# Attention and GEGLU block on one core: batch 1's queries and keys in token rows, weights in thirds, a new order in batch 0

## The chip, the cores and the metric

The kernel runs on one core of one Trainium2 chip. The metric is the device time of one execution in microseconds (us): 375.97 as the median of six runs (374.69 to 376.41). Engines are named as in the profile: PE is TensorE (PEld its weight loads), DVE is VectorE, ACT is ScalarE, POOL is GpSimd, SP is SyncE. Differences under about 0.3% are taken as no change.

## The reference

Eight batches of eight heads, 576 tokens, head size 64; each batch has 16 "beacon" keys and values that every token may see, ahead of 576 causal ones. The attention's output, put together as 4608 tokens by 512, goes through a gated block with three weight matrices.

```python
k_all = np.concatenate([beacon_k, k], axis=2)
v_all = np.concatenate([beacon_v, v], axis=2)
scores = scale * np.matmul(q, k_all.transpose(0, 1, 3, 2))
scores = np.where(causal, -1000000000.0, scores)
a = np.exp(scores - scores.max(-1, keepdims=True))
a /= a.sum(-1, keepdims=True) + 1e-09
x = np.matmul(a, v_all)                 # then transposed to (4608, 512)
g, val = x @ w_gate, x @ w_val          # (4608, 1536) each
out = (gelu(g) * val) @ w_out           # (4608, 512), float32
```

## The kernel before

All matrices are brought to bf16 by the loads themselves. GpSimd issues every load (`dma`, line 115, and the weights, lines 170 and 173), in program order, in the same queue in which it also runs its masks; SyncE issues the stores, the DMA turns of queries and keys (`transpose_dma`, line 232) and of attention output (`turn_dma`, line 365). The order of the instructions on every engine is the program's own: `keep` holds them in the order in which they are written.

**Attention of a batch.** Heads are taken in four pairs m = 0 to 3, the two heads of a pair in the two halves of the partitions. `qkT` holds turned queries and keys (head size down the partitions). For a pair, `scores` computes four chunks (0 to 3, widths 512, 480, 464, 208 a head) of keys by queries into one of two buffers of `psum_s`, and ScalarE writes their exponentials to `exp_ring`. Causal masks are added by small matmuls in batch 0 (`score_mms`, the `eye`/`neg` pairs) and made by GpSimd on the exponentials from batch 1 on (`masks`, line 292, at the end of `scores`): chunk 0 has key tile t = 0, chunk 1 tiles 2 and 4, chunk 2 tile 1, chunk 3 tile 3. `attend` (30 matmuls against values with a column of ones, x_ps) and `normalize` (DVE) follow; both together are `av`. `turn` turns the result y on TensorE and `put` copies it to `xT_sb`; pairs 0 and 1 of batches 1 to 7 are turned by DMA instead.

**The gated block.** Tokens go in nine chunks of 512. `gate_val` is one block of 128 of the 1536 columns: four matmuls for the gate and four for the value (gv_ps, 8 x 512 columns), gelu on ScalarE, product on DVE into `hT_sb`. `out_mms` accumulates the output of 128 tokens over twelve of these. Chunk b's gate/value blocks follow attention b; the output matmuls of chunk b - 1 are spread between the pieces of attention b (`o(n)` is n of them). In the last gate/value block of a chunk ("tx") the gate half is in `psum_t`, the value half in `psum_x`. The PSUM banks are `psum_s` (two buffers of two banks), `psum_x` (two banks), `psum_t` and `psum_o` (one each).

**Queries and keys.** They reach the kernel in rows of 64 elements a head and token. Batches 2 to 7 are loaded in that form (`qk_loads`, 11 loads a batch), 128 tokens to the partitions, into two rings by b % 2, and turned by DMA. Batches 0 and 1 (`NPERM` = 2) are loaded six tokens to a partition (`load_qk6`: runs of 384 elements, 96 partitions, into a buffer shared with `hT_sb`) and turned by TensorE: a half turn (`transpose_half`, w = 1 for keys, 0 for queries) is 12 turns of 96 x 64, for keys one more for the beacons, and one or two copies by DVE (by ScalarE for the first queries). Batch 1's half turns of pairs 0 to 2 stand between the gate/value blocks 5 to 10 of batch 0, that of pair 3 (`transpose_pe`) behind the first two score chunks of batch 1.

**The order around the change.** Loads: queries and keys of batch 0 by pairs; values of batch 0; gate and value weights in column blocks 0-2, 2-4, 4-8, 8-12, with the first half of batch 1's queries and keys ahead of the last of these; the second half; out weights in one load; values of batch 1. In batch 1, batch 2's 11 loads are put out in part by `ahead(2)` at two places between score chunks, the other seven behind the attention. In batch 0's attention, both half turns of a pair stand together, chunks go in twos (`c(m, *AB)` is chunks 0 and 2, `*CD` 1 and 3), two filler matmuls (`warm(2, ...)`, line 522) stand before pair 2's last two chunks, and `av` of pairs 0 to 2 stands between the chunks of pair 3.

Of the kernel before, what the change touches and what calls it, by code (L numbers as in the profile page):

```python
# [7 lines left out]
P = 128  # L8
B, H, S, NB, D = 8, 8, 576, 16, 64
SK = S + NB  # L10
# [5 lines left out]
CH = 512  # L16
N_CHUNKS = N_TOK // CH
NPAIR = H // 2
NPERM = 2
MASKED = -1e6  # L20


# [16 lines left out]
AB, CD = (0, 2), (1, 3)  # L39
# [14 lines left out]
def kernel(  # L54
# [14 lines left out]

    const = ctx.enter_context(tc.tile_pool(name="const", bufs=1))  # L70
    ring = ctx.enter_context(tc.tile_pool(name="ring", bufs=1))
    npool = ctx.enter_context(tc.tile_pool(name="npool", bufs=2))
    fpool = ctx.enter_context(tc.tile_pool(name="fpool", bufs=3))
    hpool = ctx.enter_context(tc.tile_pool(name="hpool", bufs=2))
    opool = ctx.enter_context(tc.tile_pool(name="opool", bufs=2))
# [38 lines left out]
    def dma(out_ap, in_ap):  # L114
        keep(nc.gpsimd.dma_start(out=out_ap, in_=in_ap))  # L115

    qk6 = {}

    def qk6_of(b):
        if b not in qk6:  # L120
            qk6[b] = (
                hpool.tile([P, 2, H, 6 * D], BF16, name="qk6", tag="hT_sb"),
                npool.tile([NB, H, D], BF16, name="kb", tag="kb"),
            )
        return qk6[b]

    def load_qk6(b, h0, h1, ws=(1, 0)):
        for w in ws:
            src = (q, k)[w]
            dma(  # L130
                qk6_of(b)[0][0:96, w, h0:h1, :],
                src[b, h0:h1, :, :].rearrange("h (p r) d -> p h (r d)", r=6),
            )

    def load_kb(b):
        dma(qk6_of(b)[1], beacon_k[b].rearrange("h t d -> t h d"))

    def key_loads(src, beacon, dst, b):
        parts = [
            (dst[0:NB, 0, :, :], beacon[b].rearrange("h t d -> t h d")),  # L140
            (dst[NB:P, 0, :, :], src[b, :, 0:112, :].rearrange("h p d -> p h d")),
        ]
# [4 lines left out]
        return [lambda o=o, i=i: dma(o, i) for o, i in parts]  # L147

    def qk_loads(b):
        q_sb, k_sb = q_ring[b % NRING], k_ring[b % NRING]  # L150
# [8 lines left out]
    def load_qk(b):  # L159
        for load in qk_loads(b):  # L160
            load()

    def load_v(b):
        for load in key_loads(v, beacon_v, v_ring[b % NRING][:, :, :, 0:D], b):
            load()

    def load_gate_val(f0, f1):
# [4 lines left out]
    def load_out_w():  # L172
        keep(nc.gpsimd.dma_start(out=wo_sb, in_=moe_w_out.rearrange("(ii p) m -> p ii m", p=P)))

    def mm(out_ap, lhsT, rhs, start, stop, **kw):
        keep(nc.tensor.matmul(out_ap, lhsT, rhs, start=start, stop=stop, **kw))  # L176
# [5 lines left out]
    def tr(out_ap, in_ap):  # L182
        n = in_ap.shape[0]
        keep(nc.tensor.transpose(out_ap, in_ap, ident[0:n, 0:n]))  # L184

    def tr_part(b, m, w, dst):
        qk, kb = qk6[b]
        for r in range(6):
            for hi in range(2):
                tr(  # L190
                    dst[64 * hi : 64 * hi + 64, r * 96 : (r + 1) * 96],
                    qk[0:96, w, 2 * m + hi, r * D : (r + 1) * D],
                )
        if w:
            tr(dst[:, S:SK], kb[:, 2 * m : 2 * m + 2, :])

    def transpose_pe(b, m):
        t_ps = psum_x.tile([P, 2, 1024], BF16, name="t_ps", tag="x")
        for w in range(2):
            tr_part(b, m, w, t_ps[:, w, :])  # L200
        keep(
            nc.vector.tensor_copy(
                qkT[:, m, :, NB:SK].rearrange("p w (t r) -> p w t r", r=6),
                t_ps[:, 0:2, 0:S].rearrange("p w (r t) -> p w t r", r=6),
            )
        )
        keep(nc.vector.tensor_copy(qkT[:, m, 1, 0:NB], t_ps[:, 1, S:SK]))

    def transpose_half(b, m, w, by_act=False):
        pool, tag = ((psum_o, "o"), (psum_t, "t"))[w]  # L210
        t_ps = pool.tile([P, 1024], BF16, name="t_ps", tag=tag)
        tr_part(b, m, w, t_ps)
        out_ap = qkT[:, m, w, NB:SK].rearrange("p (t r) -> p t r", r=6)
        in_ap = t_ps[:, 0:S].rearrange("p (r t) -> p t r", r=6)
        if by_act:
            act(out_ap, in_ap, ACT.Copy)
        else:
            keep(nc.vector.tensor_copy(out_ap, in_ap))  # L218
        if w:
            keep(nc.vector.tensor_copy(qkT[:, m, 1, 0:NB], t_ps[:, S:SK]))  # L220

    def warm(n, pool, tag):
        w_ps = pool.tile([P, D_MODEL], FP32, name="w_ps", tag=tag)
        for j in range(n):
            mm(w_ps, idle[:, 128 * (j % 4) : 128 * (j % 4) + 128], idle, True, True)
# [228 lines left out]
            if fi == F_TILES - 1:  # L454
                out_store(ci, ti, o_of[ci][1])

    kb_sb = opool.tile([NB, H, D], FP32, name="kb_sb", tag="o_sb")
    keep(nc.sync.dma_start(out=kb_sb, in_=beacon_k[0].rearrange("h t d -> t h d")))
    load_qk6(0, 0, 2)
    load_qk6(0, 2, 4, (1,))  # L460
    keep(
        nc.gpsimd.affine_select(
            out=eye,
# [5 lines left out]
            channel_multiplier=-1,  # L469
        )  # L470
    )
    load_qk6(0, 2, 4, (0,))
    keep(
        nc.gpsimd.affine_select(
            out=neg,
# [17 lines left out]
    load_qk6(1, 4, H)  # L493
    load_out_w()
    load_v(1)

    def av(b, m, where="x"):
# [9 lines left out]
    keep(nc.vector.tensor_copy(qk6[0][1], kb_sb))  # L507
    transpose_half(0, 0, 1)
    transpose_half(0, 0, 0, by_act=True)
# [24 lines left out]
    av(0, 3, "s")  # L534
    turn(0, 2)
    put(0, 2, by_act=True)
    keep(nc.scalar.preload_act_table_set(SET_GELU))
    gv_mms(0, 0, 0, 1)
    turn(0, 3, psum_o, "o")
    put(0, 3)  # L540
    gv_mms(0, 1, 0, 1, where="x")
    for kk in (2, 3):
        for fi in (0, 1):
            gv_mms(0, fi, kk, last=kk == 3)
    for b in range(B):
        u = [0]

        def o(n):
            out_mms(b - 1, u[0], u[0] + n)
            u[0] += n  # L550

        def ahead(n):
            for _ in range(n):
                if loads:
                    loads.pop(0)()

        loads = qk_loads(b + 1) if b == 1 else []
        if b:
            keep(nc.scalar.preload_act_table_set(SET_EXP))
            o(4)  # L560
            scores(b, (0, 0))
            scores(b, (0, 2))
            if b == 1:
                transpose_pe(1, 3)
            o(7)
            scores(b, (0, 1))
            scores(b, (0, 3), (1, 3))
            ahead(2)
            o(7)
# [24 lines left out]
            av(b, 3)  # L594
            keep(nc.scalar.preload_act_table_set(SET_GELU))
            gv_mms(b, 0, 0, 1, 2)
            gv_mms(b, 1, 0)
            turn(b, 3)
            put(b, 3)
            gv_mms(b, 1, 1, 2)  # L600
            gv_mms(b, 0, 3, last=True)
            gv_mms(b, 1, 3, last=True)
        for fi in range(F_TILES):
            if fi >= 2:
                gate_val(b, fi, "x" if b and fi == 2 else "tx" if fi == F_TILES - 1 and b < B - 1 else "s")
            if b == 0 and 5 <= fi < 11:
                transpose_half(1, (fi - 5) // 2, (fi - 4) % 2)
            if fi == 0:
                ahead(len(loads))
                if b and b + 1 < B:  # L610
                    load_v(b + 1)
                if b and b + 2 < B:
                    load_qk(b + 2)
                if NPERM <= b + 1 < B:
                    transpose_dma(b + 1)
    for fi in range(F_TILES):
        gate_val(N_CHUNKS - 1, fi)
# [37 lines left out]
```

## Time and profile before

| | |
|---|---|
| median of 6 runs | 375.97 us |
| the profiled execution | 374.69 us, span 373.0 us, granted TensorE clock 1.00 |
| TensorE busy | 364.1 us, 98% |
| GpSimd / ScalarE / VectorE busy | 158.9 / 187.8 / 152.0 us |
| DMA moved by GpSimd's queue | 19.13 MB (bf16 bytes) |
| third gate/value block of batch 0 starts | 27.06 us |
| output matmuls of chunk 0, 1, 2 start | 47.55, 87.88, 129.49 us |
| out weights: issued, landed after | 28.28 us, 17.8 us |

The span runs from the first to the last instruction. A line of the timeline gives the start, the duration, the engine, the line of the code, the operation, what it writes and reads, and in brackets the idle time before it with what ended that. Matmuls are pipelined, so a group's duration reaches some 0.17 us beyond the start of what follows; lengths of stages are better taken from start to start. From batch 3 on, one batch takes 39.72 us (129.49 to 169.21 and so on).

### The profile page before, as it was taken

The page shows a single profiled execution, that of the slowest core. Times are in us where ns is not written, and L with a number is a line of the kernel's source. Part 1 is how long each engine was busy: PE and PEld are TensorE (multiplying, and loading weights), DVE is VectorE, ACT ScalarE, POOL GpSimd, SP SyncE. Part 2 cuts the span into 40 slices and gives each one's busy share as a digit, 9 for nine tenths or more (in the row PEclk, how much of TensorE's full clock was granted, in tenths as well). Part 3 has the DMA queues.
Part 4 walks back from the last instruction along what each step waited for, and adds up shares of the span by engine and source line. Part 5 has one row for each costly group of instructions (what it writes and reads, how often), then busy time and mean ns, then how long its engine had stood idle before and what let it go on. Part 6 is the DMA issues. An engine that isn't in the chain of part 4 may idle for free.

```text
span 373.0 us, 7487 instructions
## 1 busy us (share of the span) xinstructions
PE 364.1 (98%) x3032; PEld 180.9 (49%) x3032; DVE 152.0 (41%) x257; ACT 187.8 (50%) x241; POOL 158.9 (43%) x282
## 2 busy tenths in 40 slices
PE   7899999998999999999999999999999999999996
PEld 3664445543454446444554455445544464444443
DVE  3454644442344425433444335333444244424332
ACT  4963277335753487338733774358534873332210
POOL 8935046974467245843495148614600330000000
PEclk9999999999999999999999999999999999999999
DMA  8999959999569923999299929991591030000102
GB/s 104 169 204 204 194 58 117 151 130 150 69 122 144 151 41 91 159 136 85 60 148 154 80 77 127 138 128 47 120 157 20 33 87 30 0 0 30 56 34 109
DMA packets 149826, 38.33 MB, mean 103 GB/s; under 512 B 136352, under 2 KB 145312, under 8 KB 149792
## 3 DMA queue, kind: packets, MB, share of 16 engines
q0 software_dynamic: 104960, 19.13, 68.9%
q1 hardware_dynamic: 44832, 18.73, 26.6%
q8 instruction: 24, 0.39, 0.5%
q14 instruction: 10, 0.08, 0.1%
HBM read 38.27 MB, written 9.44 MB: 128 GB/s over the span
## 4 chain that ended last, share of the span: by engine, by line
PE 89%; DMA 4%; ACT 2%; SPq 2%; POOL 1%; issue 1%; DVE 0%
PE gv_ps L176 42%; PE o_ps L176 25%; PE s_ps L176 8%; PE x_ps L176 8%; DMA qkT<-q_sb 2%; SPq L232 2%; ACT expT L179 2%; PE t_ps L184 1%; PE g_ps L176 1%; PE v_ps L176 1%; DMA k_sb<-in_k_dram 1%; PE y_ps L184 1%; PE w_ps L176 1%; POOL k_sb L115 1%; DVE y_sb L344 0%
## 5 line engine op out<-in xcount | busy, mean ns | idle before, releaser
L179 ACT ACTIVATE ge_sb<-gv_ps 128x512 bf16<-128x512 f32 x101 | 59.4, 597 | 134.2 <-PE gv_ps L176 134.2
L179 ACT ACTIVATE expT<-s_ps 128x960 bf16<-128x960 f32 (+2 forms) x114 | 101.8, 947 | 28.1 <-PE s_ps L176 24.6
L419 DVE TENSOR_TENSOR hT_sb<-gv_ps,ge_sb 128x512 bf16<-128x512 f32 x101 | 69.1, 690 | 106.2 <-ACT ge_sb L179 106.2
L176 PE MATMUL gv_ps<-xT_sb,wg_sb 128*128 128x512 bf16 x404 | 107.8, 379 | 0.0
L176 PE MATMUL gv_ps<-xT_sb,wv_sb 128*128 128x512 bf16 x404 | 107.7, 379 | 0.0
L176 PE MATMUL o_ps<-wo_sb,hT_sb 128*128 128x512 bf16 (+2 forms) x444 | 105.9, 374 | 0.0
L292 POOL TENSOR_SCALAR_AFFINE_SELECT expT<-expT 128x256 bf16<-128x256 bf16 (+2 forms) x140 | 51.7, 385 | 114.4 <-ACT expT L179 107.0
L176 PEld LDWEIGHTS <-wv_sb 128*128 128x128 bf16 x432 | 42.2, 98 | 51.0
L176 PEld LDWEIGHTS <-wg_sb 128*128 128x128 bf16 x432 | 40.8, 98 | 46.1
L176 PEld LDWEIGHTS <-hT_sb 128*128 128x128 bf16 x444 | 38.8, 98 | 46.3 <-issue 8.8
L438 DVE COPY o_sb<-o_ps 128x512 f32<-128x512 f32 (+2 forms) x37 | 25.0, 676 | 45.9 <-PE o_ps L176 45.8
L176 PE MATMUL s_ps<-qkT 64*128 64x336 bf16 (+5 forms) x384 | 35.0, 282 | 3.6 <-DMA qkT<-q_sb 1.8
L176 PEld LDWEIGHTS <-expT 128*128 128x128 bf16 (+1 forms) x960 | 32.2, 97 | 7.8 <-issue 2.3
L115 POOL DMA_DIRECT2D v_sb<-in_v_dram x40 | 33.7, 868 | 4.0 <-DMA wg_sb<-in_moe_w_gate_dram 1.6
L176 PE MATMUL x_ps<-v_sb,expT 128*128 128x65 bf16 x930 | 33.8, 193 | 0.5 <-issue 0.5
L115 POOL DMA_DIRECT2D k_sb<-in_k_dram x30 | 25.2, 846 | 20.1 <-DMA q_sb<-in_q_dram 10.8
L176 PEld LDWEIGHTS <-qkT 64*128 64x128 bf16 x384 | 14.3, 94 | 24.5 <-issue 20.8
L344 DVE TENSOR_TENSOR y_sb<-x_ps,r_sb 128x640 bf16<-128x640 f32 x31 | 25.5, 824 | 1.4 <-PE y_ps L184 0.4
L115 POOL DMA_DIRECT2D q_sb<-in_q_dram x30 | 25.4, 895 | 0.0
L342 DVE RECIPROCAL r_sb<-x_ps 128x10 f32<-128x10 f32 x31 | 6.8, 221 | 40.4 <-PE x_ps L176 40.4
L218 DVE COPY qkT<-t_ps 128x576 bf16<-128x576 bf16 x13 | 9.7, 751 | 5.9 <-PE t_ps L184 5.9
L377 DVE COPY xT_sb<-y_ps 128x576 bf16<-128x576 bf16 x16 | 7.3, 457 | 11.5 <-PE y_ps L184 11.5
(50 smaller groups left out, 120.9 us busy)
## 6 DMA issues: line engine op xcount, KB each, us to landing
out_dram<-o_sb SPq DMA_DIRECT2D x35, 256.0 KB, 2.2
v_sb<-in_v_dram POOLq DMA_DIRECT2D x24, 128.0 KB, 6.5
q_sb<-in_q_dram POOLq DMA_DIRECT2D x24, 128.0 KB, 9.3
k_sb<-in_k_dram POOLq DMA_DIRECT2D x18, 128.0 KB, 9.4
wo_sb<-in_moe_w_out_dram POOLq DMA_DIRECT2D x1, 1536.0 KB, 17.8
wg_sb<-in_moe_w_gate_dram POOLq DMA_DIRECT2D x2, 512.0 KB, 11.8
wv_sb<-in_moe_w_val_dram POOLq DMA_DIRECT2D x2, 512.0 KB, 13.8
v_sb<-in_v_dram POOLq DMA_DIRECT2D x8, 112.0 KB, 4.3
```

Source lines behind the costliest of these rows:

```text
L115: keep(nc.gpsimd.dma_start(out=out_ap, in_=in_ap))
L176: keep(nc.tensor.matmul(out_ap, lhsT, rhs, start=start, stop=stop, **kw))
L179: keep(nc.scalar.activation(out_ap, in_ap, func, **kw))
L184: keep(nc.tensor.transpose(out_ap, in_ap, ident[0:n, 0:n]))
L218: keep(nc.vector.tensor_copy(out_ap, in_ap))
L232: nc.sync.dma_start_transpose(out=qkT[:, :, w, c + j * P : c + j * P + n], in_=src[0:n, j, :, :].rearrange("p h d -> p (h d)"),)
L292: nc.gpsimd.affine_select(out=d, in_=d, pattern=[[0, 2], [1, n]], compare_op=ALU.is_ge, fill=0.0, base=NB if t == 0 else 0, channel_multip ...
L342: keep(nc.vector.reciprocal(r, x[:, :, :, D:DV]))
L344: nc.vector.tensor_tensor(out=y_sb[:, :, h0:h1, :].rearrange("p j b d -> p b j d"), in0=x[:, :, :, 0:D], in1=r.to_broadcast([P, h1 - h0, 5 ...
L377: keep(nc.vector.tensor_copy(out_ap, y_ps[:, 0:S]))
L419: nc.vector.tensor_tensor(out=h_of[ci][:, fi, :], in0=gv_of.pop((ci, fi))[1], in1=ge_sb, op=ALU.mult)
L438: keep(nc.vector.tensor_copy(o_sb[:, ti, c0:c1], o_ps))
```

## The change

- Batch 1's queries and keys are loaded as those of batches 2 to 7, in token rows (11 loads instead of five), into ring 1, behind all gate and value weights. `load_qk6` serves batch 0 alone.
- `transpose_pe` turns a pair of batch 1 by ten turns of the whole array (five for keys, beacons among them, five for queries) with one contiguous copy each by DVE. Pairs 0 and 1 stand behind gate/value blocks 9 and 10 of batch 0, pairs 2 and 3 between score chunks of batch 1. The six half turns go.
- Values of batch 0 come in two parts of four heads (11 loads instead of six), the first part ahead of pair 3's queries and keys.
- Out weights come in three loads of four blocks.
- Five of batch 2's loads are issued before the loop over batches, and two each at three places in batch 1; none is left for the end of its attention.
- In batch 0 the score chunks 1 and 3 go one by one between half turns, the filler matmuls go, `av` of pairs 0 to 2 moves behind chunks of pair 3 and gate/value matmuls go between the turns.
- `npool` has four buffers instead of two.

```diff
-    npool = ctx.enter_context(tc.tile_pool(name="npool", bufs=2))
+    npool = ctx.enter_context(tc.tile_pool(name="npool", bufs=4))
...
+    def load_qk6(m, *ws):
+        for w in ws:
+            dma(
+                qk6[0:96, w, 2 * m : 2 * m + 2, :],
+                (q, k)[w][0, 2 * m : 2 * m + 2, :, :].rearrange("h (p r) d -> p h (r d)", r=6),
...
+    def key_loads(src, beacon, dst, b, h0=0, h1=H):
+        full = dst
+        dst, src = dst[:, :, h0:h1, :], src[:, h0:h1, :, :]
+        parts = [(dst[NB:P, 0, :, :], src[b, :, 0:112, :].rearrange("h p d -> p h d"))]
...
+        loads = [lambda o=o, i=i: dma(o, i) for o, i in parts]
+        if h0 == 0:
+            loads.insert(0, lambda: dma(full[0:NB, 0, :, :], beacon[b].rearrange("h t d -> t h d")))
...
+    def load_out_w(f0, f1):
+        dma(wo_sb[:, f0:f1, :], moe_w_out[f0 * P : f1 * P, :].rearrange("(ii p) m -> p ii m", p=P))
...
+    def transpose_pe(b, m):
+        t_ps = psum_x.tile([P, 2, 1024], BF16, name="t_ps", tag="x")
+        for w, ring_, n in ((1, k_ring, SK), (0, q_ring, S)):
+            src = ring_[b % NRING]
+            for j in range(5):
+                r = min(P, n - j * P)
+                tr(t_ps[:, w, j * P : j * P + r], src[0:r, j, 2 * m : 2 * m + 2, :])
+            keep(nc.vector.tensor_copy(qkT[:, m, w, SK - n : SK], t_ps[:, w, 0:n]))
...
-    load_qk6(0, 4, 6)
-    load_qk6(0, 6, H)
-    load_v(0)
+    load_qk6(2, 1, 0)
+    load_v(0, 0, 4)
+    load_qk6(3, 1, 0)
+    load_v(0, 4, H)
     load_gate_val(0, 2)
     load_gate_val(2, 4)
     load_gate_val(4, 8)
-    load_qk6(1, 0, 4)
-    load_kb(1)
     load_gate_val(8, 12)
-    load_qk6(1, 4, H)
-    load_out_w()
+    load_qk(1)
+    for f0 in (0, 4, 8):
+        load_out_w(f0, f0 + 4)
     load_v(1)
+    loads = qk_loads(2)
...
+    ahead(5)
...
     c(0, *AB)
-    transpose_half(0, 1, 1)
-    transpose_half(0, 1, 0)
-    c(0, *CD)
-    transpose_half(0, 2, 1)
+    transpose_half(1, 1)
+    c(0, 1)
+    transpose_half(1, 0)
+    c(0, 3)
     c(1, *AB)
-    transpose_half(0, 2, 0)
+    transpose_half(2, 1)
     c(1, 1)
-    transpose_half(0, 3, 1)
+    transpose_half(2, 0)
     c(1, 3)
-    transpose_half(0, 3, 0)
     c(2, *AB)
-    warm(2, psum_x, "x")
-    c(2, *CD)
+    transpose_half(3, 1)
+    c(2, 1)
+    transpose_half(3, 0)
+    c(2, 3)
+    c(3, *AB)
     av(0, 0)
-    c(3, *AB)
+    c(3, 1)
+    c(3, 3)
     av(0, 1, "ot")
-    c(3, 1)
     av(0, 2)
-    c(3, 3)
     turn(0, 0)
+    put(0, 0, by_act=True)
+    av(0, 3, "s")
     turn(0, 1, psum_o, "o")
-    put(0, 0, by_act=True)
-    put(0, 1)
-    av(0, 3, "s")
+    put(0, 1, by_act=True)
+    gv_mms(0, 0, 0)
     turn(0, 2)
     put(0, 2, by_act=True)
     keep(nc.scalar.preload_act_table_set(SET_GELU))
-    gv_mms(0, 0, 0, 1)
+    gv_mms(0, 1, 0, where="x")
+    gv_mms(0, 0, 1)
     turn(0, 3, psum_o, "o")
     put(0, 3)
-    gv_mms(0, 1, 0, 1, where="x")
+    gv_mms(0, 1, 1, where="x")
...
             scores(b, (0, 2))
             if b == 1:
-                transpose_pe(1, 3)
+                transpose_pe(1, 2)
+            ahead(2)
             o(7)
             scores(b, (0, 1))
             scores(b, (0, 3), (1, 3))
+            if b == 1:
+                transpose_pe(1, 3)
             ahead(2)
...
-            if b == 0 and 5 <= fi < 11:
-                transpose_half(1, (fi - 5) // 2, (fi - 4) % 2)
+            if b == 0 and fi in (9, 10):
+                transpose_pe(1, fi - 9)
             if fi == 0:
-                ahead(len(loads))
```

More of the change, by code (lines that the diff above doesn't have):

```diff
@@ L18 @@
 NPAIR = H // 2
-NPERM = 2
 MASKED = -1e6
@@ L115, in dma @@
         keep(nc.gpsimd.dma_start(out=out_ap, in_=in_ap))
[L117 to L123, printed above, removed]
-            )
[L125 to L142, printed above, removed]
+    qk6 = hpool.tile([P, 2, H, 6 * D], BF16, name="qk6", tag="hT_sb")
+    kb_sb = const.tile([NB, H, D], BF16, name="kb_sb", tag="kb_sb")
+    def load_qk6(m, *ws):
[3 more added lines that the diff above has]
+                (q, k)[w][0, 2 * m : 2 * m + 2, :, :].rearrange("h (p r) d -> p h (r d)", r=6),
+            )
+    def key_loads(src, beacon, dst, b, h0=0, h1=H):
+        full = dst
+        dst, src = dst[:, :, h0:h1, :], src[:, h0:h1, :, :]
+        parts = [(dst[NB:P, 0, :, :], src[b, :, 0:112, :].rearrange("h p d -> p h d"))]
         for j in range(1, 5):
@@ L146, in key_loads @@
             parts.append((dst[0:n, j, :, :], src[b, :, r0 : r0 + n, :].rearrange("h p d -> p h d")))
-        return [lambda o=o, i=i: dma(o, i) for o, i in parts]
+        loads = [lambda o=o, i=i: dma(o, i) for o, i in parts]
+        if h0 == 0:
+            loads.insert(0, lambda: dma(full[0:NB, 0, :, :], beacon[b].rearrange("h t d -> t h d")))
+        return loads
     def qk_loads(b):
@@ L161, in load_qk, with load_v @@
             load()
-    def load_v(b):
-        for load in key_loads(v, beacon_v, v_ring[b % NRING][:, :, :, 0:D], b):
+    def load_v(b, h0=0, h1=H):
+        for load in key_loads(v, beacon_v, v_ring[b % NRING][:, :, :, 0:D], b, h0, h1):
             load()
@@ L170, in load_gate_val @@
             keep(nc.gpsimd.dma_start(out=dst[:, :, fs], in_=w[:, fs].rearrange("(kk p) f -> p kk f", p=P)))
-    def load_out_w():
-        keep(nc.gpsimd.dma_start(out=wo_sb, in_=moe_w_out.rearrange("(ii p) m -> p ii m", p=P)))
+    def load_out_w(f0, f1):
+        dma(wo_sb[:, f0:f1, :], moe_w_out[f0 * P : f1 * P, :].rearrange("(ii p) m -> p ii m", p=P))
     def mm(out_ap, lhsT, rhs, start, stop, **kw):
@@ L184, in tr, with transpose_half @@
         keep(nc.tensor.transpose(out_ap, in_ap, ident[0:n, 0:n]))
-    def tr_part(b, m, w, dst):
-        qk, kb = qk6[b]
+    def transpose_half(m, w, by_act=False):
+        pool, tag = ((psum_o, "o"), (psum_t, "t"))[w]
+        t_ps = pool.tile([P, 1024], BF16, name="t_ps", tag=tag)
         for r in range(6):
@@ L190, in tr_part @@
                 tr(
-                    dst[64 * hi : 64 * hi + 64, r * 96 : (r + 1) * 96],
-                    qk[0:96, w, 2 * m + hi, r * D : (r + 1) * D],
+                    t_ps[64 * hi : 64 * hi + 64, r * 96 : (r + 1) * 96],
+                    qk6[0:96, w, 2 * m + hi, r * D : (r + 1) * D],
                 )
         if w:
[L195 to L212, printed above, removed]
+            tr(t_ps[:, S:SK], kb_sb[:, 2 * m : 2 * m + 2, :])
         out_ap = qkT[:, m, w, NB:SK].rearrange("p (t r) -> p t r", r=6)
@@ L455, in out_mms @@
                 out_store(ci, ti, o_of[ci][1])
[L457 to L460, printed above, removed]
+    kb_in = opool.tile([NB, H, D], FP32, name="kb_in", tag="o_sb")
+    keep(nc.sync.dma_start(out=kb_in, in_=beacon_k[0].rearrange("h t d -> t h d")))
+    load_qk6(0, 1, 0)
+    load_qk6(1, 1)
     keep(
@@ L471 @@
     )
-    load_qk6(0, 2, 4, (0,))
+    load_qk6(1, 0)
     keep(
@@ L489, with ahead @@
     load_gate_val(4, 8)
-    load_qk6(1, 0, 4)
-    load_kb(1)
     load_gate_val(8, 12)
-    load_qk6(1, 4, H)
-    load_out_w()
+    load_qk(1)
+    for f0 in (0, 4, 8):
+        load_out_w(f0, f0 + 4)
     load_v(1)
+    loads = qk_loads(2)
+    def ahead(n):
+        for load in loads[:n]:
+            load()
+        del loads[:n]
+    ahead(5)
     def av(b, m, where="x"):
@@ L506 @@
     warm(8, psum_x, "x")
-    keep(nc.vector.tensor_copy(qk6[0][1], kb_sb))
-    transpose_half(0, 0, 1)
-    transpose_half(0, 0, 0, by_act=True)
+    keep(nc.vector.tensor_copy(kb_sb, kb_in))
+    transpose_half(0, 1)
+    transpose_half(0, 0, by_act=True)
     c(0, *AB)
-    transpose_half(0, 1, 1)
-    transpose_half(0, 1, 0)
-    c(0, *CD)
-    transpose_half(0, 2, 1)
+    transpose_half(1, 1)
+    c(0, 1)
+    transpose_half(1, 0)
+    c(0, 3)
     c(1, *AB)
-    transpose_half(0, 2, 0)
+    transpose_half(2, 1)
     c(1, 1)
-    transpose_half(0, 3, 1)
+    transpose_half(2, 0)
     c(1, 3)
-    transpose_half(0, 3, 0)
     c(2, *AB)
-    warm(2, psum_x, "x")
-    c(2, *CD)
+    transpose_half(3, 1)
[3 more added lines that the diff above has]
+    c(3, *AB)
     av(0, 0)
-    c(3, *AB)
+    c(3, 1)
+    c(3, 3)
     av(0, 1, "ot")
-    c(3, 1)
     av(0, 2)
-    c(3, 3)
     turn(0, 0)
+    put(0, 0, by_act=True)
+    av(0, 3, "s")
     turn(0, 1, psum_o, "o")
-    put(0, 0, by_act=True)
-    put(0, 1)
-    av(0, 3, "s")
+    put(0, 1, by_act=True)
+    gv_mms(0, 0, 0)
     turn(0, 2)
@@ L550, in o @@
             u[0] += n
[L552 to L557, printed above, removed]
         if b:
@@ L613 @@
                     load_qk(b + 2)
-                if NPERM <= b + 1 < B:
+                if 2 <= b + 1 < B:
                     transpose_dma(b + 1)
```

## The prediction

> **What bounds the kernel now.** I read the page first, then TensorE's waits, then the timeline of TensorE and of GpSimd around batches 0 to 2.
>
> The page, busy time by engine and the span in 40 slices of 9.3 us:
>
> ```profile
> span 373.0 us, 7487 instructions
> PE 364.1 (98%) x3032; PEld 180.9 (49%) x3032; DVE 152.0 (41%) x257; ACT 187.8 (50%) x241; POOL 158.9 (43%) x282
> ...
> PE   7899999998999999999999999999999999999996
> ...
> DMA  8999959999569923999299929991591030000102
> GB/s 104 169 204 204 194 58 117 151 130 150 69 122 144 151 41 91 159 136 85 60 148 154 80 77 127 138 128 47 120 157 20 33 87 30 0 0 30 56 34 109
> ```
>
> TensorE runs for 98% of the span. Only what shortens its instruction list or fills its few gaps can gain, and every new wait of TensorE costs in full. The gaps are in slices 1 to 3 (batch 0's attention) and slice 10; the DMA engines are full over the first five slices (to 46 us). TensorE's waits:
>
> ```profile
> PE s_ps L176 <- DMA qkT<-q_sb: 1.8, 1, 1.8
> PE s_ps L176 <- ACT expT L179: 0.8, 3, 0.3
> PE x_ps L176 <- issue: 0.5, 1, 0.5
> ```
>
> One wait matters: batch 2's scores wait 1.8 us for the DMA turn of batch 2's queries. The timeline of TensorE (start, duration) shows it beside batch 3's same place, and one of the six half turns of batch 1 between gate/value blocks:
>
> ```profile
> 33.10 1.03 PE L176 MATMUL gv_ps<-xT_sb,wv_sb 128*128 128x512 bf16 x4
> 34.06 0.45 PE L184 MATMUL t_ps<-eye,qk 96*64 96x96 bf16 x12
> 34.44 0.18 PE L184 MATMUL t_ps<-eye,kb 16*128 16x16 bf16 x1
> 34.55 1.04 PE L176 MATMUL gv_ps<-xT_sb,wg_sb 128*128 128x512 bf16 x4
> ...
> 87.88 1.03 PE L176 MATMUL o_ps<-wo_sb,hT_sb 128*128 128x512 bf16 x4
> 88.83 0.39 PE L176 MATMUL s_ps<-qkT 64*128 64x512 bf16 x2
> 91.00 0.37 PE L176 MATMUL s_ps<-qkT 64*128 64x464 bf16 x2 [1.77 <-DMA qkT<-q_sb]
> ...
> 129.49 1.03 PE L176 MATMUL o_ps<-wo_sb,hT_sb 128*128 128x512 bf16 x4
> 130.45 0.59 PE L176 MATMUL s_ps<-qkT 64*128 64x512 bf16 x4
> ```
>
> GpSimd issues all loads and, from batch 1 on, masks. Its timeline:
>
> ```profile
> 28.28 1.03 POOL L173 DMA_DIRECT2D wo_sb<-in_moe_w_out_dram x1 [2.89 <-DMA wv_sb<-in_moe_w_val_dram]
> ...
> 37.34 0.73 POOL L115 DMA_DIRECT2D v_sb<-in_v_dram x1 [0.62 <-DMA qk<-in_k_dram]
> 50.04 0.37 POOL L292 TENSOR_SCALAR_AFFINE_SELECT expT<-expT 128x224 bf16<-128x224 bf16 x1 [11.97 <-ACT expT L179]
> ```
>
> From 18.9 us each load waits for the landing of the load eight places before it (the load of out weights for the second of the wv loads, and so on). GpSimd is then free 12 us before the first mask of batch 1: that is the cover which the change spends.
>
> **The change part by part**, in TensorE's order, against the profiled execution (374.69 us, span 373.0; it lies 1.28 under the median of the six runs, 375.97).
>
> 1. *Batch 0's attention.* Before, the third gate/value block starts at 27.06. I laid the new order out by hand with the rows' durations: scores of a pair 0.41, 0.39, 0.46, 0.28 on TensorE, exponentials 1.02, 0.94, 0.97, 0.53 (less 0.06 overlap when back to back), a half turn 0.38 to 0.49 and its copy 0.75, attend 1.02, normalize 0.22 + 0.82, a y turn 0.27, put by ScalarE 0.65, two gate/value matmuls 0.43. Spreading the chunks keeps ScalarE fed and the two filler matmuls (0.6) go; but attends of pairs 1 to 3, all turns and gate/value then stand in a row from 17.8 us, bound by TensorE: 4 x 1.02 + 0.74 + 4 x 0.27 + 16 x 0.216 = 9.4, end 27.2. So +0.1. POOL's part: pair 3's six-row loads now stand behind six half value loads (0.53 + 5 x about 0.66, between 0.65 for a 192-run load and 0.83 for a 1024-run one), so they are issued at 9.95 and 10.6 instead of 6.11 and 6.73. With latencies of 3.3 to 5.1 (those of the first loads) they land by 13.3 to 15.1 and 13.9 to 15.7; TensorE wants them at 14.5 and 15.5. Bounds: -0.5 (the 0.5 issue gap before the last attend goes) to +1.0.
>
> 2. *Batch 1's turns on TensorE.* [...] Pair 3's turn inside batch 1 costs 0.61 (the period 47.55 to 87.88 is 40.33, the later ones 39.72). After: ten whole-array turns a pair, priced by the y turns (ten start at 20.76 and the next work at 21.29): 0.53 x 4 = 2.12. Net -1.71.
>
> 3. *A new wait on PSUM "x".* The turn of pair 1 (after block 10) sits in the bank that block 11's value half needs ("tx"). DVE copies it only after block 10's product: before, block 10's issue ends at 45.34 and that product at 46.86. Two contiguous copies follow, priced by the 128x576 copy of xT, 0.46 each, less the small overlap: released 2.35 after the block's end. TensorE wants the bank at 0.53 + 0.87 = 1.40. So +0.95 (0.7 to 1.1). For pair 0 the next turn comes 2.2 later, which just hides its copies.
>
> 4. *Do batch 1's rows land in time?* They now come in 64-element runs, behind all gate/value weights. Before, the last value load of batch 0 landed at 15.9 and the out weights at 46.1: 5776 KB in 30.2 us, 191 KB/us; batch 1's values (64-element runs) took 592 KB in 3.9 us, 150 KB/us. After: the ten half value loads are limited by their issue, the last one issued at 14.0, landing at 17.5; weights 3072 KB, 16.1 us, 33.6; rows of batch 1, 1168 KB, 7.8 us, 41.4. TensorE reaches the turn of pair 0 at 27.2 + 8 x 1.73 = 41.0 and needs the last k block. +0.4; the bounds are 0 and 2.5 (2 us of error in the chain; rows went at 130 GB/s in slice 9).
> [...]
>
> 5. *GpSimd's queue in front of batch 1's masks.* The out weights, 7.6 us by their row, land at 49.0 in thirds (first third at 44, wanted at 46; last at 49.0, wanted at about 50: hidden, by 1 us). After them come v(1) (to 52.9, wanted at 53.9) and five q loads of batch 2 that each wait for the landing eight places earlier: the second waits for the last third, so it goes at 49.3, and the queue is free at 49.3 + 3 x 0.85 + 0.7 = 52.5. Masks (0,0) and (0,2): 53.3. Two k loads (0.54 + 0.85): 54.7. Masks of (0,1) and (0,3): t=2 at 55.1, t=3 at 55.75. TensorE would start attend(1,0) at 53.85, stops at the t=2 column, then at t=3, and has 18 matmuls (0.6) left: 56.4 instead of 54.9. +1.5 (0.3 to 1.7; if step 4 is smaller, TensorE is earlier, but so is the whole chain). Pair 1's masks are ready again, at 59.6 for 60.1.
>
> 6. *Batch 2's wait.* Its q and k are all issued by 62 instead of 75 us, so SP issues the ten DMA turns without a stop, as in every later batch. The period 87.88 to 129.49 is 41.61 against 39.72: -1.89. Next late would be those same turns as batches 3 to 7 have them, and none of those waits.
>
> Deeper npool removes one 0.4 wait of DVE, off the path. Batches 3 to 7 and the tail keep their list.
>
> Sum: 0.1 - 1.71 + 0.95 + 0.4 + 1.5 - 1.89 = -0.65: 374.0 for the profiled execution, 375.3 for the median.
>
> **The rivals.**
> A. *The DMA chain runs 1.5 us earlier*: step 4 is 0 and step 5 only 0.3: -2.25, 373.7. For it: in 20 to 45 us the queue kept 204 GB/s. Against it: the half value loads leave the DMA engines short of work for some 7 us.
> B. *The other side: the chain runs 2 us later*, because rows of 64 elements go at 130 instead of 150 and the weights start late. Step 4 is 2.4, step 5 stays 1.5: +1.35, 377.3. It decides from the last k block of batch 1 landing after 43.2 us (1.8 later than reckoned). For it: five full DMA slices with no slack; against it: 191 KB/us is a mean over the same kinds of loads.
> C. *Batch 2's wait does not go*, as DMA turns now share the engines with v(2) and q/k(3) issued earlier: +1.24, 377.2. Against it: batches 3 to 7 have that same mix and no wait.
>
> **How the numbers follow.** 0.3% (1.1 us) is about what a measurement can tell from no change. My forecast, within it: 0.43, at 375.3, with its own range 374.9 to 377.0. A: 0.25. B: 0.21. C, or step 1 at its upper bound together with a late chain: 0.11. So faster 0.25, same 0.43, slower 0.32. The range 373.6 to 377.5 reaches from A to B and leaves out the tails beyond both.
>
> **What would show it.** Right: third block near 27.2; batch 1's turns as 128*128 rows, ten in some 0.53; a wait of v_ps on a DVE copy of qkT near 1 us; a short wait of t_ps on k_sb's landing near 41; x_ps or its weight load waiting for POOL masks over 1 us near 55; no wait of s_ps on qkT's DMA near 89. Wrong: a wait for k_sb of several us (B), masks on time (A), a DMA wait near 89 left (C), or ScalarE idle between 14 and 18 us for pair 3's loads.

## The result and the profile after

The changed kernel takes 379.48 us against 376.31 us for the kernel before in the runs beside it: 1.008 times as long, 95% interval 1.0063 to 1.0097. It is slower by some 3 us; no change was forecast (375.3, range 373.6 to 377.5). Single times spread over 7.4 us in the kernel before and 3.8 us in the changed one, and some of the traces show a stretch in which TensorE runs at half speed (granted clock 0.50, for 3.4 to 13.6 us), so medians and intervals are compared, and single traces only place by place.

The profiled execution of the changed kernel is 379.98 us long. Its page:

```profile
span 378.3 us, 7376 instructions
PE 366.6 (97%) x2970; PEld 183.1 (48%) x2970; DVE 149.6 (40%) x253; ACT 189.0 (50%) x242; POOL 168.8 (45%) x295
...
PE   7899879999999999999999999999999999999996
...
PEclk9589999999999999999999999999999999999999
```

TensorE has 62 instructions fewer and is busy 2.5 us longer. The line of the granted clock has a 5 and an 8 in its second and third slice, where the kernel before has nines:

```profile
PEclk9999999999999999999999999999999999999999
```

TensorE's waits (in all, times, longest) have a new first line, and the wait for batch 2's DMA turn is gone. In the names, t_ps are the turns, s_ps the scores, x_ps the attends, gv_ps, g_ps and v_ps gate and value, o_ps the output matmuls:

```profile
PE t_ps L174 <- DVE qkT L203: 4.2, 4, 1.5
PE s_ps L166 <- DVE qkT L192: 1.2, 3, 0.4
```

Stretches of 4 us of the same trace (busy time of each engine, then the granted clock, the DMA share and GB/s):

```profile
4.00:8.00 4.00, 2.98 (x53) 1.67 (x51) 0.83 (x2) 1.53 (x2) 4.00 (x7) 1.00 1.13 148
8.00:12.00 4.00, 3.52 (x53) 2.33 (x53) 1.59 (x3) 3.15 (x5) 3.99 (x7) 0.50 1.60 125
12.00:16.00 4.00, 3.59 (x57) 2.28 (x53) 1.59 (x3) 3.04 (x5) 4.00 (x7) 0.50 1.48 133
16.00:20.00 4.00, 3.59 (x57) 2.38 (x55) 1.59 (x3) 3.04 (x5) 4.00 (x6) 0.50 1.19 133
20.00:24.00 4.00, 4.00 (x102) 3.61 (x99) 1.44 (x4) 3.17 (x4) 3.28 (x5) 0.79 1.28 171
```

From 8.1 to 21.7 us the clock was 0.50. And TensorE's timeline, with the third gate/value block, the turns of pairs 0 and 1, and the places of the two predicted waits:

```profile
30.56 1.03 PE L166 MATMUL gv_ps<-xT_sb,wg_sb 128*128 128x512 bf16 x4
...
44.37 0.42 PE L174 MATMUL t_ps<-eye,k_sb 128*128 128x128 bf16 x5
46.32 0.52 PE L174 MATMUL t_ps<-eye,q_sb 128*128 128x128 bf16 x5 [1.52 <-DVE qkT L203]
46.77 1.04 PE L166 MATMUL gv_ps<-xT_sb,wg_sb 128*128 128x512 bf16 x4
...
50.90 1.04 PE L166 MATMUL g_ps<-xT_sb,wg_sb 128*128 128x512 bf16 x4
51.77 1.03 PE L166 MATMUL v_ps<-xT_sb,wv_sb 128*128 128x512 bf16 x4
52.63 1.03 PE L166 MATMUL o_ps<-wo_sb,hT_sb 128*128 128x512 bf16 x4
...
61.23 1.09 PE L166 MATMUL x_ps<-v_sb,expT 128*128 128x65 bf16 x30
...
95.10 1.03 PE L166 MATMUL o_ps<-wo_sb,hT_sb 128*128 128x512 bf16 x4
96.06 0.58 PE L166 MATMUL s_ps<-qkT 64*128 64x512 bf16 x4
```

DVE at the first turns, and GpSimd's last masks ahead of attend(1,0):

```profile
45.20 0.69 DVE L402 TENSOR_TENSOR hT_sb<-gv_ps,ge_sb 128x512 bf16<-128x512 f32 x1 [1.03 <-ACT ge_sb L169]
45.81 0.46 DVE L203 COPY qkT<-t_ps 128x592 bf16<-128x592 bf16 x1
...
58.63 1.52 POOL L275 TENSOR_SCALAR_AFFINE_SELECT expT<-expT 128x256 bf16<-128x256 bf16 x4 [0.17 <-ACT expT L169]
```

The reader is to see four things. The third block starts 3.5 us later than before (27.06). The five query turns of a pair wait 1.52 us for the copy of the keys (45.81), which DVE reaches only after the product of the block before (45.20); at pairs 2 and 3 the wait is 0.56 us. The value half of block 11 (51.77) and attend(1,0) (61.23, all 30 matmuls in one piece) wait for nothing. And at 95.10 the scores follow the output matmuls at once: batch 2's wait is gone. The next output matmuls start at 134.82, so that period is 39.72 instead of 41.61.

Start to start, the profiled pair differs by 30.56 - 27.06 = 3.50 in batch 0, by 22.07 - 20.49 = 1.58 to the output matmuls, by 42.47 - 40.33 = 2.14 in batch 1 and by -1.89 in batch 2, 5.33 in all, which is the difference of the spans (5.3). The medians differ by 3.2; the profiled execution of the kernel before had no recorded stretch of half speed, that of the changed one a long one.

### The profile page after: what moved, and what is told of

It reads as the page before. It is cut to its first block, busy times and chain, and to the rows that moved or that the text cites. A ratio compares the mean times of both kernels' runs of the same rounds, so it can differ in the third digit from the quotient of the medians.

```text
span 378.3 us, 7376 instructions
## 1 busy us (share of the span) xinstructions
PE 366.6 (97%) x2970; PEld 183.1 (48%) x2970; DVE 149.6 (40%) x253; ACT 189.0 (50%) x242; POOL 168.8 (45%) x295
## 4 chain that ended last, share of the span: by engine, by line
PE 95%; DVE 2%; DMA 1%; ACT 1%; issue 1%; POOL 0%; POOLq 0%
PE gv_ps L166 46%; PE o_ps L166 26%; PE s_ps L166 9%; PE x_ps L166 8%; PE t_ps L174 2%; PE g_ps L166 2%; PE v_ps L166 2%; PE y_ps L174 1%; DMA qk<-in_q_dram 1%; DVE qkT L192 1%; DVE qkT L203 0%; DVE hT_sb L402 0%; ACT ge_sb L169 0%; ACT expT L169 0%; POOL qk L114 0%
## 5 line engine op out<-in xcount | busy, mean ns | idle before, releaser
L114 POOL DMA_DIRECT2D k_sb<-in_k_dram x35 | 29.4, 843 | 23.3 <-DMA q_sb<-in_q_dram 10.7
L166 PE MATMUL s_ps<-qkT 64*128 64x336 bf16 (+5 forms) x384 | 37.1, 294 | 2.0 <-DVE qkT L192 1.2
L114 POOL DMA_DIRECT2D v_sb<-in_v_dram x45 | 36.7, 840 | 2.2 <-DMA wo_sb<-in_moe_w_out_dram 2.0
L114 POOL DMA_DIRECT2D q_sb<-in_q_dram x35 | 29.6, 884 | 6.5 <-DMA wo_sb<-in_moe_w_out_dram 3.1
L192 DVE COPY qkT<-t_ps 128x576 bf16<-128x576 bf16 x7 | 5.3, 757 | 10.4 <-PE t_ps L174 10.4
```

## The experiments

Theory W: the query turns' wait for the key copy. Theory P: the new order of batch 0. Rival L: batch 0's later loads. Each kernel is timed against the kernel before on its chip; ratios carry their 95% interval.

**e1: copies behind all ten turns.**

```diff
                 tr(t_ps[:, w, j * P : j * P + r], src[0:r, j, 2 * m : 2 * m + 2, :])
-            keep(nc.vector.tensor_copy(qkT[:, m, w, SK - n : SK], t_ps[:, w, 0:n]))
+        for w, n in ((1, SK), (0, S)):
+            keep(nc.vector.tensor_copy(qkT[:, m, w, SK - n : SK], t_ps[:, w, 0:n]))
```

> The changed kernel with one edit: all ten turns of a pair are issued, then both copies. Theory W (the waits inside the turns cost the time): in the changed kernel's trace the query turns wait for the key copy 1.52 us twice and 0.56 us twice, 4.2 us; these go, and the wait for the copies comes back at the bank of block 11's value half, 0.95 us as predicted in step 3. So 3.2 us less than the changed kernel: about 376.3, ratio to the kernel before 1.000. Rival P (batch 0's attention, with its half clock, is the whole loss and the waits are covered): no more than 0.5 us less, 379, ratio 1.007 or more.

Measured 377.00, ratio 1.0014 (0.9994 to 1.0034): 2.5 us less than the changed kernel's 379.48 (side by side, in the last experiment, it is 2.0). The query turns no longer wait, v_ps waits 0.56 us for a copy. Theory W holds, for 2 to 2.5 of its 3.2 us; it is not the whole loss.

**e2: the new order of batch 0 alone**, and **e3: values in halves alone**, both in the kernel before.

```diff
# e2: the lines of batch 0 from c(0, *AB) to put(0, 3) as in the change; npool bufs=4
# e3:
-    load_qk6(0, 6, H)
-    load_v(0)
+    load_v(0, 0, 4)
+    load_qk6(0, 6, H)
+    load_v(0, 4, H)
```

> The kernel before with the new order of batch 0's attention alone (chunks one by one between half turns, no filler matmuls, attends behind pair 3's chunks, four npool buffers); all loads and batch 1 stay. Theory P: the order itself lengthens batch 0 and leaves gaps in which the granted clock falls to 0.50; third gate/value block 1.5 us later at full clock and 3.5 us at half clock, so 377.8 to 379.8, ratio 1.004 to 1.009. Rival L (the later loads of values and of pair 3 do it): the order alone gives the 27.2 us of the hand walk, 376.4, ratio 1.000.

> The kernel before with one edit: batch 0's values in two halves, the first ahead of pair 3's queries and keys. Rival L: the prologue is lengthened by the loads, third block at 28 us or later and the time 1 us or more up, 377.3 or more, ratio 1.003. Theory P: pair 3's rows land in time or nearly so, within 0.5 us of the kernel before, 376.3 to 376.8, ratio 1.000 to 1.001.

Measured: e2 379.28, ratio 1.006 (1.002 to 1.0101), with six of twelve times at 375.8 to 377.8 and six at 380.7 to 382.5; e3 379.52, ratio 1.0067 (1.0039 to 1.0096). So in this round the half loads alone cost as much as theory P gave to the order; e3 was timed only this once. In e3's trace pair 3's keys are late for TensorE:

```profile
14.27 0.45 PE L186 MATMUL t_ps<-eye,qk 96*64 96x96 bf16 x12 [0.54 <-DMA qk<-in_k_dram]
```

and the third block starts at 28.57. That place does not price the loads, though: e3's trace also has half turns at half speed up to some 10 us (twelve turns in 0.62 us at 9.07, in 0.38 at 10.69), and with the loads of before such stretches alone put the third block at 27.89 (e4, 8.5 to 11.9 us) and 28.51 (f3, up to some 13 us). e2's profiled execution, at full speed after its first turns, has it at 27.98, where the hand walk had 27.2 (0.86 of it is a pause ahead of the last attend for which the trace names no releaser; in the kernel before that pause is 0.50).

**e4: step 6 alone.** Batch 2's loads early, in the kernel before.

```diff
     load_v(1)
+    loads = qk_loads(2)
+    def ahead(n): ...
+    ahead(5)
...
                 transpose_pe(1, 3)
+            ahead(2)
             o(7)
...
-                ahead(len(loads))
```

> The kernel before with step 6 alone: five of batch 2's loads issued ahead of the loop and two each at three places of batch 1, none behind its attention; batch 1 stays in six-row loads. Step 6 by itself takes the wait of batch 2's scores: 1.9 us less, 374.4, ratio 0.995, and no wait of s_ps for a DMA of qkT near 89 us. Rival: GpSimd's queue, kept busy to some 52 us, delays batch 1's masks and attend(1,0) waits 0.5 to 1.5 us at 54 us, so that only 0.4 to 1.4 us is left: 374.9 to 375.9.

> Run e4 again, beside g2 on one chip, since it had only six times. Step 6 alone: 0.987 to 0.994 of the kernel before, 372.5 to 374.4. If its first result was chance, 0.995 (the 1.9 us of the wait alone), some 374.3.

Measured 373.21, ratio 0.9904 (0.9869 to 0.9939), and again 373.30, 0.9939 (0.9902 to 0.9975). It beats both kernels. Its trace at batch 2's start:

```profile
88.71 1.03 PE L176 MATMUL o_ps<-wo_sb,hT_sb 128*128 128x512 bf16 x4
89.67 0.59 PE L176 MATMUL s_ps<-qkT 64*128 64x512 bf16 x4
90.18 1.69 PE L176 MATMUL o_ps<-wo_sb,hT_sb 128*128 128x512 bf16 x7
```

No wait, period 39.72. It keeps six-row loads for batch 1, so the queue reaches batch 1's masks with fewer loads ahead of it, and attend(1,0) does not stop. The medians moved by 3.4 and 3.2, by the ratios 3.6 and 2.3, more than the 1.9 of the wait in the profiled execution; in e2, e3 and f2, which keep that wait, it was 2.6, 2.3 and 2.5, and in f2 the seven output matmuls behind it take 3.07 us (93.23 to 96.30) instead of 1.62 as in its batch 3 (134.35 to 135.97), so that its batch 2 takes 44.00 instead of 39.72.

**f1, f2: fillers**, two matmuls ahead of chunk 0 of pairs 1 to 3, in e1 and in e2; **f3**: the kernel before without its own two. **e2r, f2r**: e2 and f2 side by side again.

```diff
+    warm(2, psum_x, "x")
     c(1, *AB)          # the same ahead of c(2, *AB) and c(3, *AB)
```

> The kernel of run e1 with two filler matmuls ahead of chunk 0 of pairs 1, 2 and 3, where TensorE stops 0.41 us (half speed) or 0.58 us (full speed) for the copy of the queries. Theory C (a half-speed stretch of TensorE, once begun, lasts to the attends because of these stops): the stretch is over by 13 us as in the kernel before, third block at 28.0 to 28.9 instead of 31.14, about 374 to 375 instead of 377.0, ratio 0.994 to 0.998. Rival D (the length of the stretch has nothing to do with the stops): the fillers only add 3 x 0.43 to 0.86 at half speed, 377.5 to 379, ratio 1.003 or more.

> The kernel of run e2 (new order of batch 0 alone) with the same six filler matmuls. e2's twelve times lie in two groups, 375.8 to 377.8 and 380.7 to 382.5. Theory C: the upper group goes, all times 375.8 to 377.8, ratio 0.999 to 1.003. Rival D: both groups stay, or the upper one alone.

> The kernel before without its two filler matmuls ahead of pair 2's last chunks. In the old order the half-speed stretch, where there is one, ends before they run (at 11.7 us in run e4, 10.6 in run e3, the fillers at 15.3 and 16.1). Theory C: no change, within 0.5 us of 376.4, ratio 0.999 to 1.001. Rival F (it is the dropped fillers that let the speed fall): an upper group near 380 appears, ratio 1.005 or more.

> Run e2 again, beside the next one on one chip. Theory C: times in two groups as before, some 376 and some 381, the upper one where TensorE stays at half speed to the attends.

> Run f2 again on the same chip as the one above. Theory C: no group at 381, all but single times below 379. Rival D (chips or chance made the difference): the same two groups as the run above.

Measured: f1 376.96 (ratio 1.0019, 0.9995 to 1.0043), f2 377.23 (1.0032, 1.0001 to 1.0063), f3 376.89 (0.9994, 0.996 to 1.0029). e2r 376.84 (1.0009, 0.9972 to 1.0046), with eleven of twelve times below 379; f2r 378.55 (1.0048, 1.0012 to 1.0085). Theory C of these runs (stops of TensorE prolong a stretch of half speed, so fillers help) fell: on one chip the fillers made e2 no faster, and e2's upper group did not come back without them. f3's interval leaves out rival F's 1.005, in the old order. The order's own part stays inconclusive: 1.006 once, 1.0009 once; and since e3 was timed only beside the first of these, the loads' part is not settled either. f1 shows something else: with batch 0 at full speed (third block at 27.46 instead of 31.14 in e1) the time stays that of e1, because the rows of batch 1 and the masks are late instead: the first pair's key turns wait 0.55 and 0.56 us for k_sb, attend(1,0) 1.36 and 0.24 us for masks, and the output matmuls after it run at half speed (58.72, four in 1.72 us instead of 0.95; granted clock 0.50 for 3.4 us from 58.8).

**g1: both parts undone.** The changed kernel with batch 0 as before and e1's copies.

```diff
# batch 0's lines from c(0, *AB) to put(0, 3) of the kernel before, copies as in e1, and
-    load_v(0, 0, 4)
     load_qk6(3, 1, 0)
-    load_v(0, 4, H)
+    load_v(0)
```

> The changed kernel with batch 0's order and value loads of the kernel before and with copies behind all ten turns: what stays is batch 1 in token rows with whole-array turns, out weights in thirds and batch 2's loads early. If batch 0 and the waits inside the turns are the whole loss, this beats the kernel before: from run e1's rows, third block to third batch 100.2 us against 102.4, so 2.2 us less plus what batch 2's wait costs in slower runs, 372.5 to 374.2, ratio 0.990 to 0.995. Rival (steps 4 and 5 of the prediction come due, now that TensorE is at the first turn at 41 us): a wait for k_sb of 0.4 and one for the masks of 0.3 to 1.5 near 54 us, 374.5 to 376, ratio 0.996 to 1.000.

Measured 374.55, ratio 0.9967 (0.9939 to 0.9995): 4.9 us less than the changed kernel's 379.48, and of the rival's waits the one for the masks has come due (the turns do not wait for k_sb). TensorE and GpSimd near 54 us:

```profile
44.34 1.04 PE L166 MATMUL g_ps<-xT_sb,wg_sb 128*128 128x512 bf16 x4
45.94 1.04 PE L166 MATMUL v_ps<-xT_sb,wv_sb 128*128 128x512 bf16 x4 [0.56 <-DVE qkT L204]
...
53.99 0.42 PE L166 MATMUL x_ps<-v_sb,expT 128*128 128x65 bf16 x8
55.33 0.39 PE L166 MATMUL x_ps<-v_sb,expT 128*128 128x65 bf16 x7 [0.92 <-POOL expT L276]
55.95 0.64 PE L166 MATMUL x_ps<-v_sb,expT 128*128 128x65 bf16 x15 [0.24 <-POOL expT L276]
56.43 1.03 PE L166 MATMUL o_ps<-wo_sb,hT_sb 128*128 128x512 bf16 x4
```

```profile
49.49 3.31 POOL L114 DMA_DIRECT2D q_sb<-in_q_dram x4 [1.70 <-DMA wo_sb<-in_moe_w_out_dram]
52.78 0.78 POOL L276 TENSOR_SCALAR_AFFINE_SELECT expT<-expT 128x224 bf16<-128x224 bf16 x2
53.47 0.56 POOL L114 DMA_DIRECT2D k_sb<-in_beacon_k_dram x1
53.99 0.86 POOL L114 DMA_DIRECT2D k_sb<-in_k_dram x1
54.82 1.42 POOL L276 TENSOR_SCALAR_AFFINE_SELECT expT<-expT 128x256 bf16<-128x256 bf16 x4
```

The attend takes 56.43 - 53.99 = 2.44 instead of 0.93: 1.5 us, as step 5 forecast, with the loads in front of the masks as the prediction listed them.

**g2: batch 2's loads behind the masks**, to show that the queue's order does it.

```diff
-    ahead(5)
+    ahead(1)
# then ahead(3) behind (0, 3) and (1, 3), ahead(4) behind (2, 0), ahead(3) behind (2, 2)
```

> The kernel of run g1 with batch 2's loads at other places of GpSimd's queue: one ahead of the loop (not five), none between the first two score chunks of batch 1 and the next two, then three, four and three behind the masks of the next groups. Theory Q (step 5: attend(1,0) stops because the masks stand behind loads that wait for landings): the stop of g1 at 54 to 56 us, 1.5 us, goes; period of batch 1 41.0 to 41.6 instead of 42.54, 373.0 to 373.6 against 374.55. Rival R (the masks are late because the exponentials or the values are): the stop stays and the time is 374.5 or more.

Measured 377.44, ratio 1.0038 (1.0001 to 1.0075): slower than g1. attend(1,0) runs in one piece (55.82, 30 matmuls), as theory Q says, but the last three loads now stand ahead of the mask of chunk (2, 3) and attend(1,2) stops:

```profile
64.47 0.54 PE L166 MATMUL x_ps<-v_sb,expT 128*128 128x65 bf16 x12 [0.16 <-POOL expT L276]
67.33 0.63 PE L166 MATMUL x_ps<-v_sb,expT 128*128 128x65 bf16 x15 [2.32 <-POOL expT L276]
```

Its profiled execution also ran at half speed (granted clock 0.50) from 8.2 to 18.4 us, with the old order of batch 0. The three loads took 2.51 us of GpSimd for their issue alone, without waiting for a landing. So the loads' place in the queue decides which attend stops; a better time was not reached this way.

**h0 to h3: the two parts side by side on one chip.**

```diff
# h0: the changed kernel; h2: e1; h3: g1
# h1: g1 with the copies of the change (inside the loop over w)
```

> The changed kernel again, for the 2 x 2 on one chip. As before: 379.5, ratio 1.006 to 1.010.

> The changed kernel with batch 0's order and value loads of the kernel before; the query turns still wait for the key copies. If the two parts add: 4.9 us lie between the changed kernel and g1, 2.5 of them the turns' wait, so batch 0 is worth 2.4 and this run gives 377.1, ratio 1.002. If they hide each other (late turns give the rows and masks time, steps 4 and 5): 375.5 to 376.5, since without batch 0's delay the waits inside the turns of pairs 2 and 3 cover the masks' 1.5 us.

> Run e1 again, beside the others: changed kernel with copies behind all ten turns. If the parts add: 2.5 us under h0, 377.0, ratio 1.001.

> Run g1 again: both parts undone. 374.5, ratio 0.995 to 0.998; a wait of the attend for batch 1's masks of 1 to 1.5 us near 54 us (step 5) in its trace, and none for the rows.

| | turns as changed | copies behind all turns |
|---|---|---|
| batch 0 as changed | h0 379.09, 1.0075 (1.0042 to 1.0107) | h2 377.13, 1.0028 (1.0003 to 1.0054) |
| batch 0 as before | h1 376.77, 1.0019 (0.9991 to 1.0048) | h3 374.83, 0.9965 (0.9942 to 0.9989) |

In the medians the parts add: 2.3 for batch 0, 2.0 and 1.9 for the turns, 4.3 for both. The traces show why taking out four waits of 4.2 us in all brings only 2: in h1, which keeps them, all 30 matmuls of attend(1,0) run in one piece (60.34), because the stops, and in this execution a slow batch 0 (third block at 29.66), give GpSimd time for the masks. In h3 the waits are gone, but v_ps waits 0.56 us for a copy and the attend stops 0.69 and 0.24 us for masks (53.69 to 55.90, 1.3 us longer than 0.93).

h0's profiled execution is the most telling trace of the changed kernel. Batch 0 ran at full speed, the third block starts at 27.45, and step 4 comes due:

```profile
41.26 0.48 PE L174 MATMUL t_ps<-eye,k_sb 128*128 128x128 bf16 x2
42.35 0.23 PE L174 MATMUL t_ps<-eye,k_sb 128*128 128x128 bf16 x1 [0.60 <-DMA k_sb<-in_k_dram]
42.76 0.23 PE L174 MATMUL t_ps<-eye,k_sb 128*128 128x128 bf16 x1 [0.18 <-DMA k_sb<-in_k_dram]
43.20 0.21 PE L174 MATMUL t_ps<-eye,k_sb 80*128 80x80 bf16 x1 [0.21 <-DMA k_sb<-in_k_dram]
43.97 0.52 PE L174 MATMUL t_ps<-eye,q_sb 128*128 128x128 bf16 x5 [0.56 <-DVE qkT L203]
```

The last key turn ends 1.7 us late; 0.76 us of this reach the next gate/value block, since the copy of the keys would have had to wait for the product anyway (first key turn to that block: 41.26 to 44.42, in the first profile 44.37 to 46.77). After that stop the clock falls (same columns as above):

```profile
42.00:44.00 2.00, 0.70 (x4) 0.33 (x5) 1.16 (x2) 0.06 (x1) 2.00 (x3) 1.00 1.17 178
44.00:46.00 2.00, 2.00 (x11) 0.97 (x11) 0.46 (x1) 0.00 (x0) 1.82 (x3) 0.79 1.11 153
46.00:48.00 2.00, 1.82 (x9) 0.87 (x7) 0.01 (x1) 0.60 (x1) 0.74 (x1) 0.50 1.11 179
48.00:50.00 2.00, 0.89 (x6) 0.54 (x6) 1.16 (x3) 0.00 (x0) 0.46 (x1) 0.50 1.24 206
```

and the output matmuls start at 52.59, where the first profile, with 3.1 us more spent in batch 0, has them at 52.63. What batch 0 gained at full speed is gone: 0.76 us at the late rows, 2.3 us in the stretch at half speed behind them (45.2 to 52.0).

## Why the prediction was wrong

**Step 3 failed, and with it step 2's view of the turns as one piece.** In the profiled pair this is the larger part of the miss; in the medians it is worth 2.0 us, about as much as batch 0. The prediction placed DVE's copies between the turns and block 11's value half and took the ten turns of a pair as one piece (step 2). Of pair 0 it said that the next turn, 2.2 us later, hides the copies. It did not ask what the second five turns wait for: they write the other half of the PSUM tile that the first copy is still to read, the trace has them wait for that copy, and the copy stands behind the product of the block before on DVE. In the kernel before `transpose_pe` issued all turns and then copied; the change itself put a copy between them. So the wait came inside every pair's turns, four times, not once at block 11: from the first key turn to the work behind the turns it is 2.40 us at pairs 0 and 1 (44.37 to 46.77) and 1.44 at pairs 2 and 3, where 0.72 would do, 4.80 us too much in all. Why the wait holds for the tile as a whole, though the halves don't overlap, no run separates. Steps 2 and 3 together were to give -1.71 + 0.95 = -0.76; the profiled pair gives 1.58 + 2.14 = 3.72. At block 11 itself nothing waits any more in the changed kernel; with the copies behind all turns (g1) the wait comes back there, v_ps starts 0.73 after its slot (45.94 instead of 45.21), where 0.95 was forecast. Shown by e1 (2.5 us), h0 against h2 (2.0) and h1 against h3 (1.9).

**Step 2's price was a little low.** Without waits a pair's ten turns take 0.72 (41.17 to 41.89 in g1), not 0.53: the five query turns take 0.45 against the keys' 0.27; why, the trace doesn't say. That is 0.8 for four pairs; -0.95 instead of -1.71. The -1.71 is 2.12 less 3.83: 0.61 for pair 3's turn and 3.22 for the six half turns (27.06 to 47.55 is 20.49, and ten blocks of 8 matmuls at 0.216 are 17.27). That is more than their own length: in the kernel before each of the six starts 0.96 after the start of the four matmuls ahead of it (33.10 to 34.06), which take 4 x 0.216 = 0.86, while the first turn of 128*128 tiles starts 0.86 after the start of the four ahead of it (43.51 to 44.37 in the first profile). What the 0.10 is, no run shows.

**Step 1 held at full speed and had no term for half speed.** Forecast +0.1, at most +1.0. At full speed h0 shows +0.4 (27.45), within the bounds; the profiled execution, at half speed for 13.6 us of batch 0, shows +3.5, and undoing batch 0's part is worth 2.3 in the median. The third block's start in the traces at hand: with the new order and loads 27.45 (h0), 30.54 (h2), 30.56 (the first profile) and 31.14 (e1); with the old order and loads, the fillers kept, 27.06 to 27.89 in five executions, 29.19 (g2) and 29.66 (h1) in two. So both orders meet slow stretches; where the recorded stretch was 10.2 us long (g2; h2 has the same mean clock, 0.986) the old order was at 29.19 (g2) and the new one at 30.54 (h2). These are too few executions to tell how often each meets one. The order and the half loads were not separated (e2, e3), and what brings the stretches on stays open. By the granted clock those at 0.50 last 13.6 us in the changed kernel (8.1 to 21.7), 10.2 in g2 (8.2 to 18.4), 3.4 in e4 (8.5 to 11.9) and 6.8 in h0 (45.2 to 52.0). TensorE's busy time does not tell the two traces of the changed kernel apart: from 3.4 to 6.8 us it was busy 2.59 us in the first profile, whose clock falls at 8.1, and 2.42 in h0, whose clock stays at 1.00 there. Whether TensorE's stops in the new order make such stretches longer was tested with fillers and not settled.

**Steps 4 and 5 were right in kind and hidden.** In the first profile TensorE reached the first turn at 44.37, not 41.0, and attend(1,0) at 61.23, 1.1 us after the last of the four masks ended (60.15). So neither wait shows. Where TensorE comes on time they do: 1.7 us for the rows in h0 (0.4 forecast, bounds 0 to 2.5), none in g1, whose value loads are those of before, and 1.5 us for the masks in g1 (1.5 forecast). Under the other losses the DMA chain was as late as rival B said: B's mark was a last key block landing after 43.2, and in the first profile it landed at about 43.8 (issued at 39.3, 4.5 us later), in h0 at about 43.2, in g1 at about 40.4 (35.8 and 4.6). So step 4's 41.4 was 2 us too early, with the half value loads. In the first profile this cost nothing, as TensorE was later still, so B did not decide the time; nor did A, whose chain was to be early, nor C, since batch 2's wait did go. (A reading of the prediction's to put right: the load of out weights waited for the third of the wv loads, the one for blocks 4 to 8, not the second; nothing rests on it.)

**Step 6 was right**: -1.89 in the profiled pair, and alone, in e4, 0.9904 and 0.9939.

With the steps as measured in the profiled pair: 3.50 + 3.72 + 0 + 0 - 1.89 = 5.33 instead of -0.65. The range missed it because it treated the DMA chain as the only large unknown; a dependence inside a moved piece, and TensorE's speed, were in no case. Without the two failed parts the sum comes close: in h3 (old batch 0, copies behind all turns) the way from the third block to the output matmuls of chunk 2 takes 101.49 us against 102.43, -0.94, where the steps as measured (-0.95 + 0.73 + 0 + 1.3 - 1.89) give -0.8.

## What to carry to other kernels

When a step is cut into alternating halves on two engines, cost the second half's start by asking which earlier reader of the same tile it must wait for and what stands ahead of that reader on its engine; issuing all writes first and all copies after was worth 2 us here, less than the waits that it removed, as others that they had covered came up. Loads put early into a queue that also runs computation are not free even when the queue looks idle: here they waited for landings and took some 0.85 us each to issue, and the masks behind them waited too, so a load's place has to be chosen mask by mask. And one part of a bundle can be worth more than the whole: early loads alone gave 0.990 and 0.994 of the time, the bundle 1.008.

## What was unexpected of the hardware

- The recorded stretches at a granted clock of 0.50 come in a few lengths (3.4 us in e4, g1 and f1, 6.8 in h0, 10.2 in g2, 13.6 in the first profile), with the old order and the new, at different places in different executions of the same code (8.1 us in the first profile, 45.2 in h0).
- The granted clock of a trace doesn't always show it. In e1's profiled execution the clock is recorded as 1.00 throughout, yet twelve turns take 0.63 us from start to start (8.32 to 8.95) instead of 0.38, and the third block starts at 31.14. In e2r, e3, f3 and h1 it is the same: from 7 to 9 us e1, e2r, e3 and f3 have 25 matmuls, the kernel before has 47 and e2 39; from 6.8 to 10.2 us h1 and e3 have 47, the kernel before has 70. The spacing of equal instructions is the safer reading.
- A stop of some 1.3 us in 2 us of TensorE (busy 0.70 of 2.00 at 42 to 44 us in h0) was followed, 1.2 us after its end, by 6.8 us at half speed (granted clock 0.50). Whether the stop brought the stretch on, no run tested.
